# Delta-rule attention with a feed-forward layer: block 4's Gram one slot later, its L loaded by SyncE, block 5's kq tied to another step

## The chip, the cores and the metric

One core of a Trainium2 chip. The metric is the device time of one execution in microseconds (us); the number for the kernel before is the median of three runs. The engines are PE (TensorE), DVE (VectorE), ACT (ScalarE), POOL (GpSimd) and SP (SyncE, which here only issues transfers).

## The reference

Four sequences, eight heads, 768 steps, head size 48. The attention is a delta rule: each head keeps a 48 x 48 state, reads it with q, and then writes the difference between v and what the state already answers to the normalised key. A feed-forward layer (FFN) of 384 to 2048 to 384 with a leaky rectifier follows.

```python
k_n = k / (np.linalg.norm(k, axis=-1, keepdims=True) + 1e-06)
for t in range(S):
    y[:, :, t] = np.einsum('bhd,bhde->bhe', q[:, :, t], state)
    v_old = np.einsum('bhde,bhd->bhe', state, kt)
    state = state + bt[:, :, :, None] * np.einsum('bhd,bhe->bhde', kt, vt - v_old)
...
h = x @ w_in
g = np.maximum(0.01 * h, h)
return (g @ w_out).astype(np.float32)
```

## The kernel before, in words

The 768 steps are cut into 12 blocks of 64. Within a block the recurrence is solved in closed form: the Gram of the keys gives a lower triangular matrix L per head and sequence, its inverse T is made by elimination, and the state is carried from block to block by matmuls. For each block there are four pieces of work, each a Python generator:

- **gram(n)** (from L275): loads kq, that is keys and queries of block n, in two tiles of two loads each (L284, on SP); multiplies them, 64 matmuls into pg (L307); ACT copies the key part to gs (L311); eight small stores bring gs to a DRAM tile gd (L315) and two loads bring it back, laid out anew, as L (L345); DVE takes the masked query part from pg as rq (L324, eight instructions). Ahead of pg stands pn, one matmul of `lengths` (L570), whose copy is nt. The stores and the load of L use one queue each time: POOL's for block 4, SP's for all others.
- **inv(b)**: the norms from L's diagonal (`norms`, L364 to L373, the first of them writes sr), then the elimination in pairs of DVE instructions (L388 and L393) on T. At its end ACT makes a transposed copy of T (L453), and SP stores both to DRAM (td at L460, tt at L461).
- **solve(n)**: reads T back (sq and rt, L520 to L529), matmuls pz, pu, pk (L619), pw, py, pc (L646) with copies on ACT between them (rt from pu at L552, rv from pc at L648); `fetch` loads k, v and q of the next block into the rings rk, rv and rq (L561 and L562); DVE scales rv by the norms (L627).
- **ffn(n)**: 16 steps f over the 2048 hidden columns. Each step has nine matmuls ph (L722, the inputs and weights are split in a high and a low part), two ACT instructions (gh at L732 and the rectified ph at L736), a DVE difference gl (L737), and six matmuls po (L713), which stand two steps behind (PD = 2). Behind the last step `columns` transposes the next block's y (px) and splits it into xh and xl.

A block has 17 slots, one per f-step and one for the end. In each slot `weave_at` takes so many steps of each generator as tables give: SV for the solve of the next block, IV for the inverse of the second next, GG and G4 for a later block's Gram. G4 has an entry for block 0, block 1 and all later blocks: first and last slot. In block 1 the Gram is that of block 4, in block 2 that of block 5.

The kernel is written for a tile framework that orders each engine's instructions itself. `behind(name)` only tells it not to plan an instruction before a marked one; on the chip it makes no wait. `mark["kq"]` is set to the second load of block 4's L, and so all later loads of kq, k, v and q are planned behind it. `mark["h2_4"]` exists too: it is set in `ffn` and names the last ACT instruction of f-step 4 of block 2. The kq tiles have two buffers (KQ_BUFS = 2), and gs has two.

Of the kernel before, what the change touches and what calls it, by code (L numbers as in the profile page):

```python
# [25 lines left out]
GS = 2  # L26
NGR = NSEQ // GS
# [20 lines left out]
def delta_moe_kernel(ctx: ExitStack, tc, kq0, kqT, kv, qT, beta, cst, w_all, out, nblk):  # L48
# [10 lines left out]
    nc = tc.nc  # L59
# [33 lines left out]
    def of(x, n, g):  # L93
        return ring[x][(n * NGR + g) % NR[x]]
# [23 lines left out]
    def behind(name):  # L118

        return tc.issue_after(mark[name]) if name in mark else nullcontext()  # L120
# [74 lines left out]
    Lh, gm, nrm, Tts, zs, ys, xs, done = {}, {}, {}, {}, {}, {}, {}, set()  # L195

    def need(gen, fn, n):
        while (fn, n) not in done:
            next(gen)
# [4 lines left out]
    def first():  # L204
# [57 lines left out]
        for n in range(2):  # L262
            for g in range(NGR):
                for y in range(2):
                    r = slice(n * 64, (n + 1) * 64)
                    with behind("dv" if n else "inverse"):
                        d = nc.vector.tensor_tensor(
                          of("q", n, g)[DN, :, y * NPAIR:(y + 1) * NPAIR], bank[g][y][r].rearrange("p (c u t) -> p c u t", c=2, u=NPAIR),
                          tri[r].rearrange("p (o v t) -> p o v t", o=1, v=1).broadcast_to([C, 2, NPAIR, C]), ALU.mult)
            after(d)  # L270
            done.add((gram, n))
            yield
# [3 lines left out]
    def gram(n):  # L276
        need(sv, solve, n - Q_BUFS // NGR)
        kqs = []
        for g in range(NGR):
            t = sb.tile([P, GS, NPAIR, 2, C], F32, tag="kq", name=f"kq{n}_{g}", bufs=KQ_BUFS)  # L280
            kqs.append(t)
            with behind("kq"):
                for b in range(2):
                    nc.sync.dma_start(t[b * R0:b * R0 + D].rearrange("p s u x t -> p (s u x t)"), kqT[n, g, b])  # L284
        if n == GS:
            yield
        b0 = where[n][0]
        Lh[b0] = sb.tile([P, HC, HC], F32, tag="L", name=f"L{b0}", bufs=2)
        gd = dr.tile([64, HC, HC], F32, tag="gd", name=f"gd{n}")
        queue = nc.gpsimd if n == GS * NGR else nc.sync  # L290
        if n - 1 > 1 and where[n - 1][0] in nrm:
            with behind("ph"):
                lengths(n - 1)
        for g in range(NGR):
            kq = kqs[g]
            gs = sb.tile([P, 2, NPAIR, C], F32, tag="gs", name=f"gs{n}_{g}", bufs=2)
            if not g:
                gm[n] = sb.tile([P, GU, HC], F32, tag="gm", name=f"gm{n}", bufs=GM_BUFS)

            ps = [ps_a.tile([P, 512], F32, tag="a", name=f"pg{n}_{g}_{b}") for b in range(2)]  # L300
            pv = [x.rearrange("p (u x t) -> p x u t", u=NPAIR, x=2) for x in ps]
            for p in range(NPAIR):
                for c in range(2):
                    for b in range(2):
                        r = slice(b * R0, b * R0 + D)
                        with behind("ph") if n > 2 else nullcontext():
                            nc.tensor.matmul(ps[b][c * 64:(c + 1) * 64, p * 128:(p + 1) * 128],  # L307
                                             kq[r, c ^ b, p, 0], kq[r, c ^ b, p].rearrange("p x t -> p (x t)"),
                                             start=True, stop=True)
            for b in range(2):  # L310
                nc.scalar.copy(gs[:, b], pv[b][:, 0])  # L311
            for c in range(2):
                for e in range(2):
                    a = e * HS + g * GH + c * GU
                    queue.dma_start(  # L315
                        gd[a:a + GU].rearrange("l j i -> j l i"),
                        gs[c * 64 + e * HC:c * 64 + (e + 1) * HC].rearrange("p b u t -> p (b u) t")[:, :, e * HC:(e + 1) * HC])

            def masked(pv=pv, qa=of("q", n, g)):
                for b in range(2):  # L320
                    for c in range(2):
                        r = slice(c * 64, (c + 1) * 64)
                        with behind("gl") if n > 2 else nullcontext():
                            nc.vector.tensor_tensor(  # L324
                                qa[DN, c, b * NPAIR:(b + 1) * NPAIR], pv[b][r, 1],
                                tri[r].rearrange("p (o t) -> p o t", o=1).broadcast_to([C, NPAIR, C]), ALU.mult)

            def corners(g=g, gs=gs):
                for c in range(2):
                    k = 2 * g + c  # L330
                    with behind("gl") if n > 2 else nullcontext():
                        nc.vector.tensor_copy(gm[n][k * HC:(k + 1) * HC].rearrange("p (b u) t -> p b u t", b=2), gs[c * 64:c * 64 + HC, :, :, HC:])

            if n == 2:
                masked()
                corners()
            elif not g:
                masked()
                held.append(corners)
            else:  # L340
                tails.extend([[masked], held + [corners]])
                held.clear()
            if g == NGR - 1:
                for r in range(2):
                    i = queue.dma_start(Lh[b0][r * 64:(r + 1) * 64].rearrange("l j i -> l (j i)"), gd.rearrange("l j i -> l (j i)"))  # L345
                if n == GS * NGR:
                    mark["kq"] = i.ins
                done.add((gram, n))
            yield
# [53 lines left out]
    def inv(b):  # L403

        if b:
            need(gg, gram, NB[b][0])
# [159 lines left out]
    def lengths(n):  # L566

        b, i = where[n]
        ps = ps_a.tile([P, 512], F32, tag="a", name=f"pn{n}")
        nc.tensor.matmul(ps[DN, 0:HS], nrm[b][i * 64:i * 64 + 64], eye0[i * 64:i * 64 + 64], start=True, stop=True)  # L570
        nt = nts[n] = sb.tile([P, NGR, 2, GU], F32, tag="nt", name=f"nt{n}", bufs=2)
        if n < 2:
            for y in range(2):
                nc.scalar.copy(nt[DN, :, :, y * NPAIR:(y + 1) * NPAIR],
                               ps[DN, y * GH:(y + 1) * GH].rearrange("p (g h v) -> p g h v", g=NGR, h=2))
        else:
            nc.scalar.copy(nt[DN].rearrange("p g h u -> p (g h u)"), ps[DN, 0:HS])
        if not n:
            for g in range(NGR):
                v = of("v", n, g)  # L580
                for u in range(GU):
                    for c in range(2):
                        nc.scalar.mul(v[DN, c, u], v[DN, c, u], nt[DN, g, c, u:u + 1])
# [190 lines left out]
    def weave_at(i, n, *streams):  # L774

        for gen, steps, a, b in streams:
            key = gen, n, a
            want = steps if i >= b - 1 else min(steps, max(0, i + 1 - a) * steps // (b - a))
            while taken.get(key, 0) < want:
                next(gen, None)  # L780
                taken[key] = taken.get(key, 0) + 1
# [5 lines left out]

    NS, NF, NI = NSLOT, NFC + 1, HC + 1
    fg, gg = first(), chain(gram, range(2, nblk))
    iv = chain(inv, range(len(NB)))  # L790
    sv = chain(solve, range(nblk))
# [45 lines left out]
    for n in range(nblk):  # L837

        for s in range(NF):
            at = min(n, 3)  # L840
            weave_at(s, n, (ff, NF, 0, NF))
            for fn, *args in work.pop(n * NF + s, ()):
                fn(*args)
            weave_at(s, n, (sv, (NS + (n == 0)) * (n + 1 < nblk), *SV[at]), (iv, NI * (n + 2 < nblk), *IV[at]),
                     (gg, NGR * (n < 2), *GG[min(n, 1)]), (gg, NGR * (0 < n < nblk - 3), *G4[min(n, 2)]))

# [2 lines left out]
WARM = {HC - 12: 16}  # L849
KA = 2  # L850
IV, GG = ((9, 17), (6, 17), (2, 17), (2, 17)), ((2, 4), (1, 2))
G4 = (0, 1), (13, 14), (12, 13)
SV = (0, 10), (3, 13), (1, 11), (2, 12)
PD, FB = 2, 4

# [65 lines left out]
```

## Time and profile before

| | us |
|---|---|
| three runs | 624.78, 621.48, 621.96 |
| median | 621.96 |
| the profiled execution | 626.66 |
| its span in the trace | 624.7 |

The profile shows one execution. An engine is busy when one of its instructions runs; the granted clock (PEclk) is the share of TensorE's full speed that was granted. A wait is given with the instruction that ended it: "2.42 <-ACT gs" is 2.42 us of idle time that ended when ACT had written gs. "issue" means that the rows show nothing that the engine waited for. The mean granted clock of the span is 0.982.

### The profile page before, as it was taken

What the parts mean: (1) busy time and instruction counts of PE and PEld (TensorE: products, weight loads), DVE (VectorE), ACT (ScalarE), POOL (GpSimd) and SP (SyncE); (2) the same over time, 40 slices, a digit from 0 to 9 for tenths busy, and PEclk for the clock granted to TensorE, in tenths of its full rate; (3) what the DMA queues carried; (4) which work ended last, traced back from release to release, by engine and by line L of the source; (5) the groups of instructions that cost most, each with busy time, mean ns of one, the idle gap of its engine ahead of it and who ended that gap; (6) DMA issues with size and microseconds to landing.
All of it is one profiled execution on the core that took longest, in us unless ns stands there. A gap on an engine that the chain in (4) does not pass through costs nothing.

```text
span 624.7 us, 22338 instructions
## 1 busy us (share of the span) xinstructions
PE 584.0 (93%) x9122; PEld 537.3 (86%) x9122; DVE 431.4 (69%) x1949; ACT 330.6 (53%) x818; POOL 39.5 (6%) x71
## 2 busy tenths in 40 slices
PE   5278989889899999999999999999999999999996
PEld 4266767688799999999999999999999999999996
DVE  3998899968648859759759739749759659331212
ACT  3377976635435536545545536545545545454432
POOL 6000000100130010010010010010010010100100
PEclk9989999989789999999999999999999999999999
DMA  5985933261470462571480570580570550500101
GB/s 127 321 249 219 290 78 79 57 115 19 98 162 9 94 135 39 104 142 24 104 149 16 112 139 19 114 149 6 117 148 7 116 94 4 87 26 4 25 1 26
DMA packets 120102, 59.69 MB, mean 96 GB/s; under 512 B 109248, under 2 KB 110336, under 8 KB 118976
## 3 DMA queue, kind: packets, MB, share of 16 engines
q1 hardware_dynamic: 116896, 52.42, 38.7%
q0 software_dynamic: 2528, 5.12, 3.3%
q8 instruction: 72, 1.18, 0.8%
q10 hardware_dynamic: 576, 0.72, 0.6%
q14 instruction: 30, 0.25, 0.1%
HBM read 46.96 MB, written 11.27 MB: 93 GB/s over the span
## 4 chain that ended last, share of the span: by engine, by line
PE 80%; DVE 13%; issue 3%; DMA 2%; ACT 1%; SPq 0%; DVEq 0%; ACTq 0%
PE po L713 31%; PE ph L722 31%; PE pk L619 3%; PE pw L636 3%; PE pg L307 3%; DVE T L393 3%; PE py L656 3%; DVE tmp L388 3%; PE pc L646 2%; DVE w L189 1%; DVE cg L175 1%; PE px L691 1%; PE pu L490 1%; PE pz L490 1%; DMA kx<-in_kq 1%
## 5 line engine op out<-in xcount | busy, mean ns | idle before, releaser
L722 PE MATMUL ph<-xh,w 128*128 128x256 f32 x1056 | 207.1, 287 | 0.0
L713 PE MATMUL po<-w,gh 128*128 128x384 f32 x704 | 179.1, 346 | 0.0
L722 PEld LDWEIGHTS ph<-xh,w 128*128 128x128 f32 x1056 | 170.3, 191 | 4.5 <-issue 3.7
L737 DVE TENSOR_TENSOR gl<-ph,gh 128x256 fp32r<-128x256 f32 x176 | 74.0, 421 | 141.6 <-ACT ph L736 135.0
L732 ACT ACTIVATE gh<-ph 128x256 fp32r<-128x256 f32 (+1 forms) x192 | 73.5, 385 | 181.4 <-PE ph L722 131.5
L722 PE MATMUL ph<-xl,w 128*128 128x256 f32 x528 | 149.3, 285 | 1.7 <-DVE xl L124 1.7
L713 PEld LDWEIGHTS po<-w,gh 128*128 128x128 f32 x704 | 122.0, 190 | 3.4 <-issue 2.0
L713 PE MATMUL po<-w,gl 128*128 128x384 f32 x352 | 113.6, 344 | 2.4 <-DVE gl L737 2.3
L393 DVE TENSOR_TENSOR T<-T,tmp 128x60 f32<-128x60 f32 (+35 forms) x661 | 112.4, 207 | 0.7
L388 DVE TENSOR_TENSOR tmp<-T,L 128x60 f32<-128x60 f32 (+35 forms) x661 | 112.1, 208 | 0.6
L722 PEld LDWEIGHTS ph<-xl,w 128*128 128x128 f32 x528 | 100.6, 191 | 2.4 <-DVE xl L124 2.1
L713 PEld LDWEIGHTS po<-w,gl 128*128 128x128 f32 x352 | 66.0, 190 | 4.0 <-DVE gl L737 3.4
L736 ACT ACTIVATE ph<-ph 128x256 f32<-128x256 f32 x176 | 66.8, 380 | 0.0
L764 POOL DMA_DIRECT2D out<-ob x44 | 23.0, 528 | 492.9 <-ACT ob L763 492.3
L324 DVE TENSOR_TENSOR rq<-pg,csb 64x256 f32<-64x256 f32 x80 | 33.8, 423 | 6.6 <-ACT gs L311 5.1
L621 ACT ACTIVATE rt<-pk 48x512 f32<-48x512 f32 x44 | 26.1, 593 | 6.3 <-PE pk L619 5.5
L648 ACT COPY rv<-pc 48x384 f32<-48x384 f32 x44 | 20.9, 475 | 13.0 <-PE pc L646 12.6
L722 PE MATMUL ph<-x,cg 128*128 128x256 f32 x96 | 22.8, 385 | 3.4 <-DVE cg L175 1.9
L638 ACT COPY rv<-pw 64x384 f32<-64x384 f32 x48 | 22.7, 474 | 6.0 <-PE pw L636 4.8
L722 PEld LDWEIGHTS ph<-x,cg 128*128 128x128 f32 x96 | 17.7, 190 | 8.1 <-DVE cg L175 3.4
L307 PE MATMUL pg<-kq 48*64 48x128 f32 x640 | 24.0, 284 | 0.0
L636 PEld LDWEIGHTS pw<-rv,rt 128*32 128x32 f32 x1536 | 19.0, 114 | 5.3 <-ACT ph L736 2.1
(101 smaller groups left out, 610.1 us busy)
## 6 DMA issues: line engine op xcount, KB each, us to landing
wr<-in_w_all SPq DMA_DIRECT2D x8, 1536.0 KB, 14.2
kq<-in_kqT SPq DMA_DIRECT2D x40, 192.0 KB, 4.8
rk<-in_kv SPq DMA_DIRECT2D x24, 192.0 KB, 3.8
rv<-in_kv SPq DMA_DIRECT2D x24, 192.0 KB, 3.9
rq<-in_qT SPq DMA_DIRECT2D x24, 192.0 KB, 3.7
L<-gd SPq DMA_DIRECT2D x18, 256.0 KB, 4.3
out<-ob POOLq DMA_DIRECT2D x44, 96.0 KB, 2.5
td<-T SPq DMA_DIRECT2D x40, 64.0 KB, 3.0
```

The lines of the kernel that those rows point to most:

```text
L307: nc.tensor.matmul(ps[b][c * 64:(c + 1) * 64, p * 128:(p + 1) * 128], kq[r, c ^ b, p, 0], kq[r, c ^ b, p].rearrange("p x t -> p (x t)"), s ...
L324: nc.vector.tensor_tensor(qa[DN, c, b * NPAIR:(b + 1) * NPAIR], pv[b][r, 1], tri[r].rearrange("p (o t) -> p o t", o=1).broadcast_to([C, NP ...
L388: nc.vector.tensor_tensor(tv, t[:, :, j:j + 1].broadcast_to([P, k, w]), L[:, j, j + 1:].rearrange("p (o w) -> p o w", o=1).broadcast_to([P ...
L393: mark["steps"] = nc.vector.tensor_tensor(t, t, tv, ALU.subtract).ins
L621: nc.scalar.mul(t[UP, c], pv[c * 64:c * 64 + D].rearrange("p (y v) t -> p y v t", y=2), -1.0)
L636: nc.tensor.matmul(pv[a:a + HC, u], t[:, c, u // NPAIR, u % NPAIR, e * HC:(e + 1) * HC], v[:, c, u], start=True, stop=True)
L713: i = nc.tensor.matmul(po[t][:, :DO], a[:, ts_], w, start=(f == 0 and k == 0), stop=(f == NFC - 1 and k + 1 == len(ways)))
L722: i = nc.tensor.matmul(ph, w[:, cc * P:(cc + 1) * P], a, start=(k == 0), stop=(k + 1 == len(ways)))
L732: i = nc.scalar.activation(gh, ph, AF.Prelu, alpha=0.01)
L736: i = nc.scalar.activation(ph, ph, AF.Prelu, alpha=0.01)
L737: mark["gl"] = nc.vector.tensor_tensor(gl, ph, gh.bitcast(F32), ALU.subtract).ins
L764: nc.gpsimd.dma_start(out[r0:r0 + C], ob[a:a + C])
```

## The change

```diff
-            with behind("kq"):
+            with behind("h2_4" if n == GS * NGR + 1 else "kq"):
                 for b in range(2):
                     nc.sync.dma_start(t[b * R0:b * R0 + D].rearrange("p s u x t -> p (s u x t)"), kqT[n, g, b])
...
-                    i = queue.dma_start(Lh[b0][r * 64:(r + 1) * 64].rearrange("l j i -> l (j i)"), gd.rearrange("l j i -> l (j i)"))
+                    i = nc.sync.dma_start(Lh[b0][r * 64:(r + 1) * 64].rearrange("l j i -> l (j i)"), gd.rearrange("l j i -> l (j i)"))
...
-G4 = (0, 1), (13, 14), (12, 13)
+G4 = (0, 1), (14, 15), (12, 13)
```

GS * NGR is 4. So block 4's Gram is woven into slot 14 of block 1 in place of slot 13; the two loads of its L are issued by SP, while its eight gd stores stay on POOL; and kq of block 5 is planned behind the fifth f-step of block 2 in place of behind the load of block 4's L. The framework plans every engine's order anew, and a few places move.

PE at the end of block 1, where the solve's pc ends (pn is the matmul of `lengths`, pg the Gram, ph the first FFN product). The difference:

```order
 L646 MATMUL pc_0_2472<-rv_84,rk_76 48x48 x16
 L646 MATMUL pc_1_2491<-rv_85,rk_77 48x48 x16
-L570 MATMUL pn_2571<-csb,sq_2059 64x32
-L307 MATMUL pg_0_0_2577<-kq_0_2563 64x128 x8
 L722 MATMUL ph_73<-xh_1_1725,w_1747 128x256
 L722 MATMUL ph_73<-xh_2_1729,w_1747 128x256
```

The Gram left this place. Of the change, a little further on PE, behind the second FFN product of f-step 12:

```order
L713 MATMUL po_0_1788<-w_1745,gh_12_2461 128x384 x2
L713 MATMUL po_0_1788<-w_1745,gl_12_2463 128x384
L713 MATMUL po_1_1789<-w_1745,gh_12_2461 128x384 x2
L713 MATMUL po_1_1789<-w_1745,gl_12_2463 128x384
L570 MATMUL pn_2618<-csb,sq_2059 64x32
L307 MATMUL pg_0_0_2624<-kq_0_2610 64x128
L307 MATMUL pg_0_1_2625<-kq_0_2610 64x128
```

It now stands here in one piece, 13 ph and these six po later. On DVE, the eight rq of this Gram move with it, from ahead of T's last steps to ahead of the next block's xl; on ACT, T's copy comes ahead of the gs copies.

SP, around the last loads of block 5's kq (the two lines ahead of the added ones), the difference:

```order
 L284 DMA kq_0_3455<-in_kqT 48x1024
 L284 DMA kq_1_3458<-in_kqT 48x1024 x2
+L345 DMA L_2616<-gd_2617 64x1024 x2
+L561 DMA rv_84<-in_kv 64x768
+L562 DMA rq_78<-in_qT 48x1024
+L561 DMA rv_85<-in_kv 64x768
+L562 DMA rq_79<-in_qT 48x1024
 L360 DMA cb_4653<-in_beta 128x32
```

L's loads came from POOL, those of block 3's rv and rq from an earlier place on SP, ahead of td; kq did not move.

DVE in block 2, around the first instructions that read block 4's L (sr and rc are the norms, gl_3 to gl_5 the differences of f-steps 3 to 5). Before:

```order
L737 TENSOR_TENSOR gl_3_2892<-ph_73,gh_3_2890 128x256
L737 TENSOR_TENSOR gl_4_2927<-ph_72,gh_4_2925 128x256
L364 TENSOR_SCALAR sr_2867<-L_2569 128x32
L365 TENSOR_SCALAR sr_2867<-sr_2867 128x32
L367 RECIPROCAL rc_2868<-sr_2867 128x32
L737 TENSOR_TENSOR gl_5_2963<-ph_72,gh_5_2961 128x256
```

Now:

```order
L737 TENSOR_TENSOR gl_3_2892<-ph_73,gh_3_2890 128x256
L364 TENSOR_SCALAR sr_2867<-L_2616 128x32
L365 TENSOR_SCALAR sr_2867<-sr_2867 128x32
L367 RECIPROCAL rc_2868<-sr_2867 128x32
L368 SCALAR_TENSOR_TENSOR rc_2868<-rc_2868,L_2616 128x32
L369 SCALAR_TENSOR_TENSOR sr_2867<-sr_2867,rc_2868 128x32
L367 RECIPROCAL rc_2868<-sr_2867 128x32
L737 TENSOR_TENSOR gl_4_2927<-ph_72,gh_4_2925 128x256
```

Six instructions of the norms, the first of which reads L, moved from behind gl_4 to ahead of it.

## Rows read from the trace of the kernel before

**Rows 1.** The page's busy times of the whole span, us (share) xinstructions:

```profile
PE 584.0 (93%) x9122; PEld 537.3 (86%) x9122; DVE 431.4 (69%) x1949; ACT 330.6 (53%) x818; POOL 39.5 (6%) x71
```

**Rows 2.** The page's chain that ended last, shares by engine:

```profile
PE 80%; DVE 13%; issue 3%; DMA 2%; ACT 1%; SPq 0%; DVEq 0%; ACTq 0%
```

**Rows 3.** Stretches: us, busy of PE, PEld, DVE, ACT, POOL, PEclk, DMA, GB/s:

```profile
161.20:163.40 2.20, 0.04 (x3) 0.03 (x2) 2.20 (x20) 0.00 (x0) 0.00 (x0) 1.00 0.60 143
165.40:170.80 5.40, 5.40 (x57) 4.85 (x56) 2.21 (x7) 2.20 (x5) 0.94 (x2) 0.50 0.79 166
170.80:175.70 4.90, 4.90 (x19) 4.90 (x18) 2.37 (x6) 1.96 (x6) 2.60 (x5) 0.50 0.90 146
175.70:178.30 2.60, 2.60 (x18) 2.56 (x18) 2.09 (x8) 1.02 (x3) 0.88 (x2) 1.00 0.33 53
```

**Rows 4.** Timeline of PE: start, us, engine line op out<-in xcount [idle before <-releaser]:

```profile
163.37 0.97 PE L646 MATMUL pc<-rv,rk 128*48 128x48 f32 x34 [2.16 <-issue]
...
167.18 3.68 PE L307 MATMUL pg<-kq 48*64 48x128 f32 x48
...
178.32 0.28 PE L722 MATMUL ph<-xh,w 128*128 128x256 f32 x1
...
193.11 1.99 PE L619 MATMUL pk<-rt,rk 64*48 64x64 f32 x64
```

**Rows 5.** Stretch of another Gram, tile pg alone, columns as in rows 3:

```profile
214.50:216.60 2.10, 2.04 (x64) 1.83 (x64) 0.00 (x0) 0.05 (x1) 1.00 0.21 34
```

**Rows 6.** Timeline of ACT and DVE at the end of block 1:

```profile
163.65 1.96 ACT L648 COPY rv<-pc 48x384 f32<-48x384 f32 x4 [2.75 <-PE pc L646]
...
166.24 0.86 DVE L324 TENSOR_TENSOR rq<-pg,csb 64x256 f32<-64x256 f32 x2 [2.42 <-ACT gs L311]
...
167.75 1.06 ACT L453 COPY T<-T 128x512 f32<-128x512 f32 x1 [1.54 <-DVE T L393]
```

**Rows 7.** Timeline of SP's queue, issues:

```profile
159.74 1.00 SPq L562 DMA_DIRECT2D rq<-in_qT  x2
...
167.75 0.86 SPq L460 DMA_DIRECT2D td<-T  x2
...
180.92 1.50 SPq L284 DMA_DIRECT2D kq<-in_kqT  x3
```

**Rows 8.** Timeline of POOL, issues of gd and L:

```profile
169.86 1.79 POOL L315 DMA_DIRECT2D gd<-gs  x3 [51.65 <-ACT gs L311]
...
177.43 1.17 POOL L315 DMA_DIRECT2D gd<-gs  x2 [2.17 <-issue]
...
181.90 1.09 POOL L345 DMA_DIRECT2D L<-gd  x2
```

**Rows 9.** The page's DMA issues: xcount, KB each, median us from issue to landing:

```profile
kq<-in_kqT SPq DMA_DIRECT2D x40, 192.0 KB, 4.8
...
L<-gd SPq DMA_DIRECT2D x18, 256.0 KB, 4.3
...
L<-gd POOLq DMA_DIRECT2D x2, 256.0 KB, 7.2
gd<-gs POOLq DMA_DIRECT2D x8, 32.0 KB, 2.9
```

**Rows 10.** Timeline of DVE, in block 2 and in another block:

```profile
188.95 0.42 DVE L737 TENSOR_TENSOR gl<-ph,gh 128x256 fp32r<-128x256 f32 x1 [2.73 <-ACT ph L736]
189.67 0.19 DVE L364 TENSOR_SCALAR sr<-L 128x32 uint32<-128x32 uint32 x1 [0.30 <-DMA L<-gd]
...
372.07 0.19 DVE L364 TENSOR_SCALAR sr<-L 128x32 uint32<-128x32 uint32 x1 [3.56 <-DMA L<-gd]
...
373.97 0.22 DVE L368 SCALAR_TENSOR_TENSOR rc<-rc,L 128x32 f32<-128x32 f32 x1
```

**Rows 11.** Timeline of ACT in block 2:

```profile
189.41 0.38 ACT L732 ACTIVATE gh<-ph 128x256 fp32r<-128x256 f32 x1 [0.49 <-DVE gl L737]
...
190.09 1.50 ACT L552 COPY rt<-pu 32x256 f32<-32x256 f32 x4
```

## The prediction

> **What bounds the kernel now.** I read the busy times first: PE is busy for 584.0 of the 624.7 us of the span, DVE for 431.4, the others less [rows 1]. The chain that ended last agrees: 80% of it is PE, 2% DMA [rows 2]. So time is saved only where PE idles, runs at half its clock, or waits. The second view is the table of stretches around the end of block 1, where the change acts [rows 3]: 161.2 to 163.4 holds no instruction of PE that is busy (0.04 us), and then the granted clock is 0.50 of 2.4 GHz, that is 1.2 GHz, from 165.44 to 175.68, between stretches at 1.00. PE's own list has the same gap of 2.16 us ahead of the 34 pc matmuls, and the 48 last pg matmuls of block 4's Gram taking 3.68 us [rows 4]; the same 64 in another block run in 2.10 at full clock [rows 5]. Everything that PE did in these 10.24 us would have taken half the time at most, so the half-rate stretch costs up to 5.1 us. It is the one place near the change where there is something to win. Block 2's ffn begins at 178.32, and pk, the first matmuls of block 3's solve, start at 193.11 [rows 4].
>
> The profiled execution took 626.66 us; the median of the runs is 621.96, which is 4.70 less, and the runs spread over 3.30 (621.48 to 624.78). That is about the price of one such half-rate stretch, so I take it that some runs pay less for it than the profiled one. A measurement of this kernel can tell about 0.5% from no change, 3.1 us.
>
> **The Gram one slot later (G4).** The order of PE's instructions has pn and the 64 pg behind 13 ph and the 6 po of f-step 12, no longer between pc and ph. Nothing is added on PE, and its work behind pc is then dense ffn. Their end moves: pc ends at 164.34 [rows 4], 13 ph by 0.28 (the row at full clock) are 3.6, 6 po of 384 columns by 0.28 x 384/256 are 2.5, the 64 pg 2.1 [rows 4, 5]: 172.5 where it was 170.86, so 1.7 later, if the clock holds. So gs and its stores gd come 1.7 later. On DVE, T's last steps no longer stand behind the first rq pair, which took 0.86 after waiting 2.42 for gs [rows 6]. ACT copies T at 167.75 after an idle time of 1.54 that ended with DVE's T [rows 6]; it can come forward by no more than those 1.54, and I take 1.4. The same on SP, whose td at 167.75 heads everything up to kq's last loads at 180.92 [rows 7]: kq at 179.5, and free at 181.0 instead of 182.42. All eight rq of the Gram (8 by 0.43 from the pair [rows 6]) now stand right ahead of the xl of the next block on DVE: 3.4 us into a stretch of 4.90 in which DVE was busy 2.37 [rows 3], so up to 0.9 late; I take 0 because T's steps have left it, and keep 0.9 for the range. What PE gets back at the end of block 1 lies between 0 and 5.1; whether it is used is decided in block 2.
>
> **L of block 4 on SyncE.** POOL loses two issues of 0.55 each behind the stores of out [rows 8]; POOL is on no chain, 0. SP gains two of about 0.5, placed behind kq's last loads. They need every gd store landed: the last one started at 178.0 [rows 8], 1.7 later is 179.7, and with the 2.9 that such a store takes [rows 9] 182.6. From there a load of L takes 4.3 on SP's queue (median of 18) and took 7.2 on POOL's (median of 2) [rows 9]. So L lands between 185.9 (SP free at 181.0, second issue 181.6, 4.3, were gd no obstacle) and 189.8 (182.6 + 7.2); I take 182.6 + 4.3 = 186.9, since the 18 rows are of just this queue. Before, sr, which reads L, began at 189.67, the end of a wait for L [rows 10]. POOL or SP, the row says 2.9 us between the queues. The Trainium skill, "DMA: Bandwidth & Descriptors" (Specifications, and Rules for kernel authors), has the two kinds of queue on the same 16 engines, with first bytes after about 1 us from GpSimd and 0.6 from SyncE: by it 0.4 us would be won, not 2.9. An L load of 6.8 from 182.6 would land at 189.4 and give +0.4 instead of the -2.0 below; no row here shows both queues under the same load, which is why the trace does not rule this out.
>
> **What now waits for L.** The order of DVE puts sr and the norm steps behind it ahead of gl_4, where they stood behind it. So gl_4 waits for L, and with it ACT's gh_5, which started 0.04 after gl_4's end, and the rt copies behind it that pk needs [rows 10, 11]. After L: the six instructions from sr on end where the second row of L368 begins in another block, 372.07 to 373.97 [rows 10], that is 1.90 with a gl among them, for which I take off 0.35, so 1.55; then gl_4 0.42 [rows 10]; then from gh_5's start at 189.41 to the end of rt at 191.59, 2.18 [rows 11]. pk can't start before L + 4.15. With 186.9 that is 191.1; it was 193.11. So of what PE wins ahead (0 to 5.1) only 2.0 is kept, and the rest turns into a wait. From the ends of L: 185.9 gives 190.05, a gain of 3.1; 189.8 gives 193.95, a loss of 0.8. That DVE waits so is not new: in the other block sr waited 3.56 for L [rows 10].
>
> **kq of block 5 behind the fifth step of block 2.** The gate only orders the planner; in SP's order these loads stay where they were, ahead of L. They are needed at 214.5 [rows 5] and take 4.8 [rows 9]: landed by 187, some 27 us early. Cost 0; were the L load held back for a first quarter of them, 0.5 (1.50/3 [rows 7]).
>
> **The loads of block 3's rv and rq** leave the place ahead of td on SP (two rq issues, 1.00, at 159.74 [rows 7]) for the place behind L. They land by about 182.6 + 4 x 0.5 + 4.8 = 189.4 with the largest load time of this queue; rv is scaled after gl_5, which waits for gh_5, so not before 190. Cost 0, bound 0.5. The 2.16 gap on PE had no releaser in the rows; the rq loads ran in it (143 GB/s [rows 3]), so it could shrink by anything from 0 to 2.2. I take 0: pc waits for ACT copies, not for rq.
>
> **The sum** against the profiled execution: 626.66 - 2.0 = 624.66, range of this case -3.1 to +0.8, with 0.9 more if rq delays xl. The median holds less of the half-rate stretch; I take two thirds of the gain, 1.3: **620.7 us**.
>
> **The rivals.**
> *A, all of it comes back.* L lands by 184 or the planner's order doesn't bind, and PE runs from pc to pk at full clock. Then 621.96 - 5.1 = 616.9. For: the 10.24 us at 0.50 are plainly there, and SP issues earlier. Against: gd lands at 182.6. Chance 0.16.
> *B, nothing comes back.* The gap of 2.16 stays, so the clock falls as before, or the timed runs hardly have the stretch; and L at 186.9 + 4.15 lies ahead of 193.1, so that it doesn't matter. Then 622.4: the median and 0.4 for rq or L. For: the gap has no cause that the change clearly removes, and the median is 4.70 below the profile. Chance 0.22. The Trainium skill, "TensorE: Matmul & The Clock Gate" (What's actually happening), says that one kernel shows other numbers of slow matmuls from run to run; the spread of 3.30 agrees with that, and it speaks for B.
> *C, slower.* PE arrives at pk 5.1 early, and waits 3.1 for gl_4 and rt in the middle of block 2. After its idle time of 2.16 at 161.2 the clock stood at 0.50 for 10.24 us [rows 3, 4]; the same again costs 5.1, on top of the forecast: 625.8. It decides from the point where the wait in block 2 gets as long as that earlier one: pk at 190.2 with all 5.1 won, so L at 186.0 or later. Against: matmuls of other f-steps stand ahead of pk and break the wait up, and all 5.1 must be won first. Chance 0.17, of which 0.12 lies over the bound of 625.1.
> *That the change does not do what it says* holds for its third part, as told: kq's place does not move. The time is the same.
>
> **How the numbers follow.** The forecast's case has 0.45: 0.08 of it below 618.85 (L at 185.9 and the gap shrunk), the rest inside. Faster: 0.08 + 0.16 = 0.24. Slower: 0.12. Same: 0.64. The range goes from A, 616.9, less 0.1 for A's own scatter, to 624.8, which takes in the loss of 0.8 with 0.9 and the slowest of the runs before (624.78), and leaves out most of C and half of A, 0.20.
>
> **What would show it.** Right: granted clock near 1.00 behind 165; T's copy on ACT near 166.4; L landing near 187 with sr waiting for it and gl_4 behind it; a wait of PE for gl or rt just ahead of pk of block 3, in sum under 3.1; pk near 191. A would show pk near 188 without a PE wait; B the clock at 0.50 at the end of block 1 as before; C a second stretch of 0.50 between 185 and 200. The forecast is wrong if L lands later than 189.8, or if anything outside block 1's end and block 2's first half moves by over 1 us.

## The result: slower, by a wait in block 2 and the half clock behind it

The changed kernel took 626.93 us (median of 9 runs, 623.71 to 631.32) against 621.92 (9 runs, 621.12 to 625.71): ratio 1.0071, 95% interval 1.0041 to 1.0100. The forecast was 620.7 with a range up to 624.8, so it was wrong in sign and in range; what came is rival C, priced at 625.8. A second set of twelve runs of the same order (the changed kernel once more, below) gives 1.0039: both intervals exclude no change, and the size lies between 0.1% and 1.0%.

The page of the changed kernel, busy times and the chain that ended last, beside [rows 1, 2]:

```profile
PE 586.0 (93%) x9122; PEld 538.3 (86%) x9122; DVE 430.9 (68%) x1949; ACT 330.2 (52%) x818; POOL 38.4 (6%) x69
...
PE 74%; DVE 13%; ACT 4%; DMA 3%; issue 3%; SPq 1%; POOL 1%; DVEq 0%; ACTq 0%
```

PE's own work is the same to 2.0 us, but 6% of the chain have left PE and stand at ACT, DMA, POOL and SP's queue: PE now waits for something. Where is read from PE's list (start, us, instruction, idle time ahead of it and what ended it), beside [rows 4]:

```profile
166.20 0.97 PE L646 MATMUL pc<-rv,rk 128*48 128x48 f32 x34 [1.34 <-issue]
167.10 0.51 PE L722 MATMUL ph<-xh,w 128*128 128x256 f32 x2
...
168.75 0.51 PE L713 MATMUL po<-w,gh 128*128 128x384 f32 x2
...
169.90 0.24 PE L570 MATMUL pn<-csb,sq 64*64 64x32 f32 x1
...
170.04 1.98 PE L307 MATMUL pg<-kq 48*64 48x128 f32 x61
...
190.30 0.28 PE L722 MATMUL ph<-xh,w 128*128 128x256 f32 x1
194.18 2.72 PE L619 MATMUL pk<-rt,rk 64*48 64x64 f32 x64 [3.60 <-ACT rt L552]
...
212.62 1.64 PE L646 MATMUL pc<-rv,rk 128*48 128x48 f32 x64
```

The pg matmuls run at full clock (1.98 for 61, where the last 48 took 3.68), and pk waits 3.60 for rt. This profiled execution reached pc 2.83 later than the one of before and not by the change, since PE's order is the same up to there (it has 17.07 us at half clock in its first 60 us, the other 6.83), so the two are compared from pc, as distances. From the second piece of pc to pk: 194.18 - 166.20 = 27.98, before 193.11 - 163.37 = 29.74. From pk to the next pc: 18.44, where before had 15.44, by this row of before's list:

```profile
208.55 1.64 PE L646 MATMUL pc<-rv,rk 128*48 128x48 f32 x64
```

So PE won 1.76 up to pk and lost 3.00 behind it. What it lost there is the clock. Stretches of the changed kernel (us, busy of PE, PEld, DVE, ACT, POOL, PEclk, DMA, GB/s):

```profile
184.00:188.00 4.00, 4.00 (x41) 3.55 (x40) 0.00 (x0) 0.66 (x2) 0.00 (x0) 1.00 1.04 260
188.00:192.00 4.00, 2.58 (x21) 2.37 (x19) 1.12 (x5) 0.00 (x0) 0.00 (x0) 1.00 0.99 225
192.00:196.00 4.00, 1.82 (x52) 1.82 (x54) 3.80 (x13) 3.17 (x10) 0.00 (x0) 0.90 0.03 10
196.00:200.00 4.00, 4.00 (x28) 3.85 (x25) 3.90 (x21) 2.77 (x7) 0.00 (x0) 0.50 0.03 4
```

Behind the wait the granted clock is 0.50 (1.2 GHz) from 195.24 to 202.06; at the end of block 1, where before had 0.50 for 10.24 us [rows 3], it is 1.00. The half clock moved from the one place to the other. Who made PE wait is read backwards through DVE, ACT and SP, first DVE's and then ACT's and SP's lists of the changed kernel:

```profile
190.75 0.19 DVE L364 TENSOR_SCALAR sr<-L 128x32 uint32<-128x32 uint32 x1 [7.13 <-DMA L<-gd]
...
192.32 0.36 DVE L737 TENSOR_TENSOR gl<-ph,gh 128x256 fp32r<-128x256 f32 x1
```

```profile
192.71 0.38 ACT L732 ACTIVATE gh<-ph 128x256 fp32r<-128x256 f32 x1 [6.39 <-DVE gl L737]
...
193.40 1.49 ACT L552 COPY rt<-pu 32x256 f32<-32x256 f32 x4
```

```profile
182.45 1.47 SPq L284 DMA_DIRECT2D kq<-in_kqT  x3
184.23 1.13 SPq L345 DMA_DIRECT2D L<-gd  x2
```

L is issued right behind kq's last three loads, lands at 190.75, and sr, gl_4, gh_5, rt and pk follow in 3.43 us. DVE stood idle for 7.13 and ACT for 6.39: in [rows 10, 11] these were 0.30 and 0.49.

### The profile page after: what moved, and what is told of

It is laid out like the page before. It is cut to its first block, busy times and chain, and to the rows that moved or that the text cites. A ratio compares the mean times of both kernels' runs of the same rounds, so it can differ in the third digit from the quotient of the medians.

```text
span 629.4 us, 22334 instructions
## 1 busy us (share of the span) xinstructions
PE 586.0 (93%) x9122; PEld 538.3 (86%) x9122; DVE 430.9 (68%) x1949; ACT 330.2 (52%) x818; POOL 38.4 (6%) x69
## 4 chain that ended last, share of the span: by engine, by line
PE 74%; DVE 13%; ACT 4%; DMA 3%; issue 3%; SPq 1%; POOL 1%; DVEq 0%; ACTq 0%
PE ph L722 29%; PE po L713 28%; PE pk L619 3%; PE pw L636 3%; DVE T L393 3%; DVE tmp L388 3%; PE py L656 3%; PE pc L646 3%; PE pg L307 2%; DMA L<-gd 2%; DVE w L189 1%; PE px L691 1%; DVE rq L324 1%; ACT cg L168 1%; DMA kx<-in_kq 1%
## 5 line engine op out<-in xcount | busy, mean ns | idle before, releaser
L722 PE MATMUL ph<-x,cg 128*128 128x256 f32 x96 | 24.5, 408 | 2.4 <-DVE cg L175 2.2
L619 PEld LDWEIGHTS pk<-rt,rk 64*48 64x48 f32 x704 | 20.9, 123 | 6.5 <-ACT rt L552 3.8
L619 PE MATMUL pk<-rt,rk 64*48 64x64 f32 x704 | 22.6, 221 | 3.6 <-ACT rt L552 3.6
L722 PEld LDWEIGHTS ph<-x,cg 128*128 128x128 f32 x96 | 19.2, 205 | 7.6 <-DVE cg L175 3.4
```

Of the source, the lines that this page charges most:

```text
L619: nc.tensor.matmul(pv[r, u], k[DN, c, u], t[DN, c, u // NPAIR, u % NPAIR], start=True, stop=True)
L722: i = nc.tensor.matmul(ph, w[:, cc * P:(cc + 1) * P], a, start=(k == 0), stop=(k + 1 == len(ways)))
```

## The experiments

Theory W is that wait: L lands late behind kq, the norms stand ahead of gl_4, and PE pays the wait and then the clock. The rivals are S (the first 60 us, which differ from execution to execution, made the difference) and G (the Gram at slot 14 costs something itself).

**The third edit alone.** On the kernel before:

```diff
-            with behind("kq"):
+            with behind("h2_4" if n == GS * NGR + 1 else "kq"):
```

> Only the third edit (kq of block 5 behind the fifth step of block 2) on the kernel before. Theory W (the changed kernel loses by the wait of pk for rt in block 2, 3.60 us, which comes from L through sr, gl_4 and gh_5, and by the 6.83 us at half clock behind it): this edit alone moves no instruction, so the time is that of before, ratio 0.998 to 1.002, and the profile shows whether the half-rate stretch at the end of block 1 (165 to 176 us in the profile of before) comes again in the same order of instructions. Rival S (the profiled difference is mostly the first 60 us, where the changed kernel's profile has 17.07 us at half clock against 6.83): the same time too, but a scatter of several us between executions of one order.

624.34 us against 623.19 (35 runs of before, 619.63 to 628.63), ratio 1.0022 (0.9996 to 1.0047). No instruction moves, so this is the kernel before once more, and the interval holds no change. Its profile has a half-rate stretch at the end of block 1 again, but 6.83 us long, not 10.24, and 28.36 from pc to pk. The scatter of several us that S speaks of is real, on either side of every comparison.

**The first edit alone.** On the kernel before:

```diff
-G4 = (0, 1), (13, 14), (12, 13)
+G4 = (0, 1), (14, 15), (12, 13)
```

> Only the first edit (block 4's Gram at slot 14); L stays on POOL. PE has the order of the changed kernel, but on DVE sr and the norms stand behind gl_5 and the scaling of rv. Theory W: nothing ahead of pk waits for L, so pk follows ph without a gap, no half-rate stretch in block 2, and all of the 5.4 us that PE won at the end of block 1 stays: 616.5 to 620, ratio 0.991 to 0.997. Rival G (the Gram at slot 14 itself costs, by the eight rq ahead of xl or by the later gd): slower than before, 623 to 627, with waits of PE ahead of block 2's ph or at block 4's solve. Rival S: 621.9, no change.

621.65, ratio 0.9979 (0.9957 to 1.0002). PE's list:

```profile
162.85 0.97 PE L646 MATMUL pc<-rv,rk 128*48 128x48 f32 x34 [1.61 <-issue]
...
187.15 1.99 PE L619 MATMUL pk<-rt,rk 64*48 64x64 f32 x64
```

POOL's and DVE's:

```profile
179.35 1.09 POOL L345 DMA_DIRECT2D L<-gd  x2
```

```profile
187.63 0.19 DVE L364 TENSOR_SCALAR sr<-L 128x32 uint32<-128x32 uint32 x1 [1.07 <-DMA L<-gd]
```

24.30 from pc to pk, with no wait and no half clock, so G falls. L came no earlier than in the changed kernel, at pc + 24.78 (187.63), but only sr waits for it, which the planner had put behind gl_5 here. The time missed what was expected: 621.65 lies above all of 616.5 to 620, and the interval just holds no change. 5.4 us in the profile are 1.5 in the medians.

**The second edit alone.** On the kernel before:

```diff
-                    i = queue.dma_start(Lh[b0][r * 64:(r + 1) * 64].rearrange("l j i -> l (j i)"), gd.rearrange("l j i -> l (j i)"))
+                    i = nc.sync.dma_start(Lh[b0][r * 64:(r + 1) * 64].rearrange("l j i -> l (j i)"), gd.rearrange("l j i -> l (j i)"))
```

> Only the second edit (L of block 4 on SP, with kq of block 5 planned behind it); the Gram at slot 13. The norms stand ahead of gl_3 on DVE. Theory W: the end of block 1 is as before, PE comes to block 2 late enough that L is there: L issued at about 181, landed by 185.5 to 187, and gl_3, which stood at 185.8, is held by 0 to 3 us; PE loses 0 to 2 us: 621.9 to 624, ratio 1.000 to 1.004. Rival S and rival G: no change, 621.9.

624.74, ratio 1.0021 (0.9999 to 1.0043): inside W's ratio, but the interval also holds the no change of S and G, so that the time does not decide. The rows show the wait that W had: PE waits twice ahead of pk, in all 1.95, and the clock stays at 1.00:

```profile
184.94 0.44 PE L713 MATMUL po<-w,gl 128*128 128x384 f32 x1 [1.12 <-DVE gl L737]
...
188.87 1.99 PE L619 MATMUL pk<-rt,rk 64*48 64x64 f32 x64 [0.83 <-ACT rt L552]
```

**The first and second edit, without the third.** On the changed kernel:

```diff
-            with behind("h2_4" if n == GS * NGR + 1 else "kq"):
+            with behind("kq"):
```

PE, DVE, ACT and POOL keep the changed kernel's order word for word; on SP, L stands ahead of kq.

> First and second edit; kq of block 5 stays behind L as in the kernel before, so that SP issues L ahead of kq's loads. All other engines have the changed kernel's order. Theory W: L is issued 1.5 to 2 us earlier than in the changed kernel and has the queue to itself, so it lands 2 to 3.5 us earlier; pk's wait of 3.60 falls to 0.1 to 1.6, too short for the clock to fall: 617 to 621, ratio 0.990 to 0.998. If the wait stays over 2 us and the clock falls all the same: 624 to 626. Rivals S and G: as the changed kernel, 625 to 627.

621.54, ratio 0.9974 (0.9948 to 1.0001): inside the ratio of W, half a microsecond above its 617 to 621. SP's, DVE's and PE's lists:

```profile
177.49 1.14 SPq L345 DMA_DIRECT2D L<-gd  x2
...
181.14 2.17 SPq L284 DMA_DIRECT2D kq<-in_kqT  x4
```

```profile
183.08 0.19 DVE L364 TENSOR_SCALAR sr<-L 128x32 uint32<-128x32 uint32 x1 [3.44 <-DMA L<-gd]
```

```profile
162.25 0.97 PE L646 MATMUL pc<-rv,rk 128*48 128x48 f32 x34 [1.62 <-issue]
...
186.54 1.99 PE L619 MATMUL pk<-rt,rk 64*48 64x64 f32 x64
```

L is there at pc + 20.83, and pk at pc + 24.29 waits for nothing, though DVE still waits 3.44. With the first two edits in place, it is the third that makes the change slow: this interval and those of the changed kernel (from 1.0041, and from 1.0009 below) do not meet.

**The changed kernel once more,** with the gate at another step, which moves nothing:

```diff
-            with behind("h2_4" if n == GS * NGR + 1 else "kq"):
+            with behind("h2_9" if n == GS * NGR + 1 else "kq"):
```

> The changed kernel with the gate of block 5's kq at the tenth step in place of the fifth (h2_9), which moves no instruction on any engine: the changed kernel once more, on the chip of the runs before it. Theory W: pk of block 3 waits for rt again, 3 to 4 us, because L is behind kq's 576 KB on SP; a stretch at half clock follows in this profile too; the time is 625 to 628, ratio 1.002 to 1.008. Rival S (the first profile's 17 us at half clock in the first 60 us made the difference): the time is that of before, 622 to 624, and the wait, if there, costs nothing.

626.18 against 623.94, ratio 1.0039 (1.0009 to 1.0070). Its first 60 us have 10.24 us at half clock, near those of before, and yet:

```profile
163.14 0.97 PE L646 MATMUL pc<-rv,rk 128*48 128x48 f32 x34 [1.34 <-issue]
...
190.89 3.65 PE L619 MATMUL pk<-rt,rk 64*48 64x64 f32 x64 [3.38 <-ACT rt L552]
...
209.29 1.64 PE L646 MATMUL pc<-rv,rk 128*48 128x48 f32 x64
```

The wait is there again (3.38), and so is the half clock behind it: 18.40 from pk to the next pc, and in the stretches

```profile
188.00:192.00 4.00, 1.11 (x22) 1.11 (x24) 3.76 (x13) 2.48 (x8) 0.00 (x0) 0.81 0.37 84
192.00:196.00 4.00, 4.00 (x53) 3.86 (x50) 3.87 (x18) 2.87 (x8) 0.00 (x0) 0.50 0.02 4
```

SP's and DVE's lists:

```profile
181.12 1.13 SPq L345 DMA_DIRECT2D L<-gd  x2
```

```profile
187.46 0.19 DVE L364 TENSOR_SCALAR sr<-L 128x32 uint32<-128x32 uint32 x1 [6.91 <-DMA L<-gd]
```

L's issue is at pc + 17.98 (181.12), where the run without the third edit had pc + 15.24, and it lands 3.49 later (187.46, that is pc + 24.32): 2.74 of it from the issue, the rest from a load that takes longer: its second half 5.77 from issue to landing, 5.02 in the run without the third edit.

**The norms behind gl_5.** On the changed kernel, in the weaver, so that block 4's norms come three slots later to the planner:

```diff
             want = steps if i >= b - 1 else min(steps, max(0, i + 1 - a) * steps // (b - a))
+            want = min(want, 1) if gen is iv and n == 2 and i < 5 else want
```

> The changed kernel with block 4's norms (sr and what follows) handed to the planner three slots later, so that on DVE they stand behind gl_5 and the scaling of rv; kq stays ahead of L on SP, PE's order is the same. Theory W: L lands as late as in the changed kernel, but pk does not wait for it, no half clock behind it; 620 to 622.5, ratio 0.995 to 0.999, and 4 to 6 below the changed kernel. Rival S: no difference from the changed kernel. If L's late landing costs by itself (the elimination of block 4 ends later): 623 to 625.

621.48, ratio 0.9954 (0.9922 to 0.9985). L is issued as late as in the changed kernel and DVE reads it at pc + 23.89, but pk waits for nothing. PE's, SP's and DVE's lists:

```profile
163.33 0.97 PE L646 MATMUL pc<-rv,rk 128*48 128x48 f32 x34 [1.62 <-issue]
...
187.65 1.99 PE L619 MATMUL pk<-rt,rk 64*48 64x64 f32 x64
```

```profile
181.26 1.13 SPq L345 DMA_DIRECT2D L<-gd  x2
```

```profile
187.22 0.19 DVE L364 TENSOR_SCALAR sr<-L 128x32 uint32<-128x32 uint32 x1 [0.16 <-DMA L<-gd]
```

S falls with it: beside the same 35 runs of before the changed kernel is 4.70 slower than this one, and the two intervals do not meet.

**The second and third edit, without the first:**

```diff
-G4 = (0, 1), (14, 15), (12, 13)
+G4 = (0, 1), (13, 14), (12, 13)
```

> Second and third edit without the first: the Gram at slot 13, L on SP behind kq's loads, the norms ahead of gl_4. Theory W: PE comes to pk later than in the changed kernel, since it runs the pg matmuls ahead of ph, and L lands about as in the run with the second edit alone plus 2 us: wait of 1.5 to 3.5 ahead of pk; 624 to 627, ratio 1.001 to 1.006. Rival G (the Gram at slot 14 costs): 622 to 623.5.

628.12, ratio 1.0081 (1.0048 to 1.0114), more than expected. The wait ahead of pk is the longest of all:

```profile
193.44 3.65 PE L619 MATMUL pk<-rt,rk 64*48 64x64 f32 x64 [4.24 <-ACT rt L552]
```

Behind it the clock is 0.50 for 6.83 us. The first edit does not make the loss. By the distances it makes it smaller (from pc to the next pc 46.15 and 46.42 with it, 48.42 without); the intervals of the ratios overlap.

**L ahead of kq and the norms late,** the edits of the fourth and the sixth run together.

> First and second edit, and the norms three slots later: L ahead of kq and nothing ahead of pk waits for it. Theory W: the run with the first and second edit had no wait of PE there already, so nothing is left to win: within 1 us of 621.5. If gl_4's place had a hidden price, 1 to 2 below that.

621.43, ratio 0.9964 (0.9936 to 0.9991), 24.32 from pc to pk: nothing left to win there, as expected.

**Half of kq ahead of L.** On the changed kernel:

```diff
-            with behind("h2_4" if n == GS * NGR + 1 else "kq"):
+            with behind("h2_4" if n == GS * NGR + 1 and not g else "kq"):
```

> The changed kernel with two of kq's four loads for block 5 ahead of L on SP and two behind it; no other engine's order changes. A dose between the changed kernel (four ahead, wait of pk 3.4 to 3.6) and the run with the first and second edit (none ahead, no wait). Theory W: L is issued about 1 us earlier and has 384 KB less ahead of it, so it lands 1.5 to 2.5 us earlier and pk waits 0.9 to 2.1 us; if a wait of that length leaves the clock at 1.00, 621.5 to 624, about the wait above the run without it; if it falls, 624 to 626.5. Rival S: no difference from the changed kernel.

623.75 against 622.86, ratio 1.0007 (0.9981 to 1.0034), between the two:

```profile
182.93 0.19 DVE L364 TENSOR_SCALAR sr<-L 128x32 uint32<-128x32 uint32 x1 [4.66 <-DMA L<-gd]
```

```profile
186.37 1.99 PE L619 MATMUL pk<-rt,rk 64*48 64x64 f32 x64 [1.14 <-ACT rt L552]
```

A wait of 1.14, and the clock stays at 1.00 from 46.88 to 616.9.

**The pg matmuls in turn.** On the kernel before, block 4's 64 matmuls planned one behind another, so that the two row halves alternate:

```diff
-                        with behind("ph") if n > 2 else nullcontext():
-                            nc.tensor.matmul(ps[b][c * 64:(c + 1) * 64, p * 128:(p + 1) * 128],
+                        with tc.issue_after(mark["pg"]) if n == 4 and p + c + b else behind("ph") if n > 2 else nullcontext():
+                            mark["pg"] = nc.tensor.matmul(ps[b][c * 64:(c + 1) * 64, p * 128:(p + 1) * 128],
...
-                                             start=True, stop=True)
+                                             start=True, stop=True).ins
```

> The kernel before with the 64 pg matmuls of block 4's Gram planned one behind another in the order that they are written, so that the two halves of the rows alternate; the planner then puts them behind ph of f-step 12 by itself, at slot 13, with L on POOL. Theory: of the 1.45 us by which the stretch from pc to pk is shorter with the Gram at slot 14 (at full clock 24.3 against 25.8 less its waits), about 1 comes from pg: 16 of one half each took 1.06 and 48 alternating ones 1.96. Then all 64 take 2.1 here, the stretch from pc to pk is 24.3 to 25 at full clock, and the time is 621.5 to 623. If the slot and not the alternation counts, 25.5 to 26 and no change of time.

622.72, ratio 0.9986 (0.9962 to 1.0009): the time can't tell. The rows can. In the run without the first edit, at a clock of 1.00, and here:

The last matmul of a row takes 0.27 by itself, which the row holds.

```profile
164.52 1.06 PE L307 MATMUL pg<-kq 48*64 48x128 f32 x15
...
166.54 1.96 PE L307 MATMUL pg<-kq 48*64 48x128 f32 x48
```

```profile
166.31 1.97 PE L307 MATMUL pg<-kq 48*64 48x128 f32 x62
```

There the first 16 are of one half, and so are 16 of the 48; all in turn, 62 take what 48 took there. From pc to pk it is 26.90, with 0.64 of a new wait for xl and a half-rate stretch of 3.41 in it, so about 24.6 without them: the alternation explains most of the 1.45 (25.7 to 25.8 for the old order at a clock of 1.00 and less its waits, in the runs with the second edit alone and with the second and third, against 24.3), and the slot need not be 14.

The runs in one table. Distances in us are from the lists of PE and DVE of each profile: the start of sr and of pk from the second piece of pc, the idle time of PE ahead of pk (in the third run two waits, in the last one the wait for xl), and from pk to the next pc. Each ratio is to the runs of before that were taken beside it, whose medians are 621.92 for the changed kernel, 623.19 for the next four rows, 623.94 for the four from "changed again" on and 622.86 for the last two; times of different groups are compared by their ratios.

| run | pc to sr | pc to pk | PE's wait | pk to pc | median us | ratio |
|---|---|---|---|---|---|---|
| before | 26.30 | 29.74 | 0 | 15.44 | 621.92 | |
| changed | 24.55 | 27.98 | 3.60 | 18.44 | 626.93 | 1.0071 |
| third edit | 24.54 | 28.36 | 0 | 15.55 | 624.34 | 1.0022 |
| first edit | 24.78 | 24.30 | 0 | 15.71 | 621.65 | 0.9979 |
| second edit | 23.07 | 27.79 | 1.95 | 15.79 | 624.74 | 1.0021 |
| first and second | 20.83 | 24.29 | 0 | 15.83 | 621.54 | 0.9974 |
| changed again | 24.32 | 27.75 | 3.38 | 18.40 | 626.18 | 1.0039 |
| norms late | 23.89 | 24.32 | 0 | 15.44 | 621.48 | 0.9954 |
| second and third | 25.69 | 29.95 | 4.24 | 18.47 | 628.12 | 1.0081 |
| first, second, norms late | 23.76 | 24.32 | 0 | 16.10 | 621.43 | 0.9964 |
| half of kq ahead | 22.08 | 25.52 | 1.14 | 16.11 | 623.75 | 1.0007 |
| pg in turn | 26.34 | 26.90 | 0.64 | 15.57 | 622.72 | 0.9986 |

Wherever PE's wait was 3.38 to 4.24, a stretch at half clock followed it (three of three) and pk to pc took 18.4; with waits up to 1.95 none did (three of three), and it took 15.6 to 16.1.

## Why the prediction was wrong

**The gain ahead: right, at its upper end.** "Between 0 and 5.1": PE was through with all that stands ahead of pk at 194.18 - 3.60 = 190.58, pc + 24.38, where before it was pc + 29.74, so 5.36. But it is not all clock. The old order at a clock of 1.00 (the run with the second and third edit) comes to 29.95 - 4.24 = 25.71, so about 4.0 is the clock and 1.4 the order, most of it pg in turn; the text had put the order at nothing.

**SP's chain: right.** kq's last loads were to come 1.4 earlier; from pc they came at 16.25 instead of 17.55, 1.30 earlier.

**The place of the Gram and gd: wrong.** The sum let pg end 1.7 later, with 13 ph by 0.28 and six po by 0.42. These are the times of single matmuls, and matmuls overlap: the 13 ph took 168.75 - 167.10 = 1.65 in all and the six po 169.90 - 168.75 = 1.15, 2.8 instead of 6.1. So pg ended at pc + 5.82, where before it was pc + 7.49: 1.67 earlier. gd was then no obstacle, and L went out right behind kq.

**L's landing: 1.0 too early, by two errors against each other.** 186.9 in the time of before is pc + 23.5; it was 24.55. The load started 0.6 earlier than the 182.6 that gd was to set (its second issue at pc + 18.60, 181.97 in the time of before), and took longer. The second load of L took 190.75 - 184.23 - 0.57 = 5.95, not the median of 4.3 [rows 9], between the two rows. Of the Trainium skill's two figures for a first byte ("DMA: Bandwidth & Descriptors", Specifications) no run here shows a separate price: from POOL in the first edit's run, L was read at pc + 24.78, from SP behind kq at pc + 24.32, from SP ahead of kq at pc + 20.83. From its second issue to its landing L took 7.73 on POOL there and 7.22 in the profile of before, with kq's loads under way from SP at the same time; on SP it took 5.39 to 5.95 behind all of kq, and 4.51 and 5.02 ahead of it (the runs with the second edit alone and with the first and second). So both seem to count: the queue by 1.3 to 2.3 (on POOL the four stores of out also stood ahead of L), and kq ahead of it by 0.4 to 1.4 and by the 2.74 of the later issue.

**What waits for L: right.** L + 4.15 was forecast for pk, 3.43 measured; a gain of 2.0 at pk, 1.76 measured; a wait of up to 3.1, 3.60 measured.

**The step that failed is the weight given to rival C.** The sum ended at pk, with "the rest turns into a wait". The wait was in the forecast's own main case, up to 3.1 us just ahead of pk, longer than the 2.16 after which the clock had fallen in [rows 3, 4]; by C's own condition, L at 186.0 or later, the forecast's L at 186.9 was past it. The sum put the clock behind that wait at nothing. The prediction spoke against C with matmuls of other f-steps that would break the wait up. They stand ahead of pk in PE's order, and so they had run: nothing was left to fill the wait. With all 5.1 won, the forecast had to hold C's clock, which it left to a rival of 0.17. Its price was too high, 5.1 for a stretch as long as that of before; the stretch was 6.83, and 3.00 was lost by the distances. That alone turns the 2.0 gained into about 1.0 lost: -1.76 + 3.00 = +1.24 between the two profiles. That C's 625.8 lies so near what came is in part luck: its clock was 2.1 too dear, and the 620.7 under it, which was to hold a wait, is about what the new order takes without one (0.9954 to 0.9979 of 621.92 are 619.1 to 620.6).

**"Cost 0" for the third edit is the other step that failed.** That kq's place on SP does not move was right, and it hid what the edit does. With L on SP the old gate, L's own load, would have put kq behind L; the new one puts it back in front. The comparison to make was with the first two edits, not with the kernel before. It costs 3.49 in L, and 4.64 between the medians (626.18 and 621.54, of two groups of runs whose before differ by 0.75, so 3.89 less that).

**The step from the profile to the median was too generous.** Two thirds of the gain were to show in the runs. The old order has the half-rate stretch at the end of block 1 in two of four profiles (10.24 and 6.83 us, and none in the runs with the second edit alone and with the second and third), so the median holds only a part of it, while the wait in block 2 came in both profiles of the changed order. So beside the median of before, the loss is larger than the 1.24 between the profiles. Without that wait, the new order is worth 0.2% to 0.5% (the four runs with a ratio under 0.998), not 5.4 us. That speaks for the reason given in rival B, and the Trainium skill's sentence there ("TensorE: Matmul & The Clock Gate", What's actually happening) agrees with these four profiles at that place. The four do not settle it: the two with a stretch are also the two with L on POOL and the rq loads in the gap, the two without have L on SP, and pg in turn, with L on POOL, has a stretch of 3.41; so the second edit may itself take the stretch away. What speaks for chance is that the mean clock of single runs spreads from 0.980 to 0.993 with the second edit alone too.

What the changed order loses again is seen in each run's mean clock: its median is 0.984 in the second set of runs of the changed order and 0.9905 with the norms late. Over 625 us that is 2 x 0.0065 x 625 = 8.1 us more at half clock, near the 6.83 of the stretch behind the wait. It is worth 4 us of the 4.70 between them at most, and 2.3 to 3.3 by straight lines laid through the three groups of runs of before, in which a run is 3.5 to 5.0 us longer for each 0.010 of mean clock lost. That leaves 0.6 to 2.4 for the wait, less than the 3.38 of the profile; the two profiled executions differ by 6.02, so a typical run pays less than the profiled one, and how much of it is wait was not measured.

Left open is why the end of block 1 falls to half clock in some executions: the gap ahead of the second piece of pc is in every profile, 1.34 to 2.16 us, also where no fall follows, and its cause was not tried.

With the Gram at slot 14, the versions with L ahead of kq, or with the norms behind gl_5, have lower ratios than both kernels; for the two with the norms late the interval excludes no change (0.9954, to 0.9985, and 0.9964, to 0.9991).

## What to carry to other kernels

When a change makes the engine that bounds a kernel arrive early somewhere, look for what it will then wait for, and price the wait together with what the clock did after a wait of that length in the same trace. If an instruction that waits for a transfer is planned ahead of one that the bounding engine needs, try moving it behind: with the norms behind gl_5 it cost nothing here and made L's late landing harmless. And when one edit changes what another is tied to, compare it with the change less that edit: an edit that seems to move nothing may be undoing what its neighbour did.

## What the runs showed of the hardware that was not expected

The 48-row pg matmuls start twice as often when their two row halves (partitions from 0 and from 64) alternate: 62 took 1.97 us and 15 in a row of one half took 1.06, both at a clock of 1.00. Less the 0.27 of the last one, that is one start every 28 ns against one every 56 ns.

The same program's executions spread over 9 us, 619.63 to 628.63 in 35 runs, and the longer ones have the lower mean clock (correlation -0.79), as stretches at half clock that come and go would make it: in the first 60 us the profiles of all these kernels have between 6.83 and 17.07 us of it.
